# A new instruction order for a fused attention and expert kernel: first values by a casting load, gate steps split from the weight loads, just-in-time loads

## The chip, the cores and the metric

The kernel runs on one core of one Trainium2 chip. The metric is the time of one execution on the device in microseconds (us). Each comparison below runs the kernels on the same chip, beside the kernel before, and states the median and the ratio to the kernel before with its 95% interval. Runs over 1.5% above the fastest of the same kernel are classed slow; the ratios and all profiles are of fast runs alone, while a median can hold a slow run. The profiled run of a kernel has a span that is about 1.6 us shorter than its time (215.1 against 216.68 in the kernel before).

## The reference, cut to what matters

```python
# q, k, v: (8, 8, 576, 64)   w_gate: (512, 8)   w1: (8, 512, 1024)   w2: (8, 1024, 512)
scores = q @ k.T / sqrt(64)                   # per batch and head
mask   = (rel >= 0) & (rel < 64)              # sliding window of 64, causal
attn   = softmax(where(mask, scores, -1e9)) @ v
x      = attn.transpose(0, 2, 1, 3).reshape(8, 576, 512)
e      = argmax(x.mean(axis=1) @ w_gate)      # one expert for a whole batch
out[b] = gate_prob[b] * (relu(x[b] @ w1[e]) @ w2[e])
```

The expert of a batch is known only when the attention of that batch is complete. A batch's expert weights (2 MB for w1 and as much for w2, as fp32) can then be loaded, and only then can its expert matmuls run. So the kernel runs the attention of later batches between the expert matmuls of earlier ones.

## The kernel before

Each engine's order of instructions follows one list of tokens. A "unit" is one fifth of a batch's attention (number = 5 x batch + part; part 4 is the tail of 64 positions). `T` transposes q and k, `U` and `k` copy the transposes out of PSUM (`a` on ACT, `d` on DVE), `S` makes scores (`b`: the mask is added by matmuls; otherwise `K` multiplies by it on DVE), `E` exponentiates on ACT, `l` sums on TensorE, `n` and `R` make the reciprocal on ACT, `A` multiplies by the values and `X` scales on DVE. `g` and `G` make the gate, `H` and `I` its probability. `Q`, `t`, `L` load q/k, tails and values of a batch through the GpSimd queue, `c` is the next expert chunk (most are 8 matmuls of 512 columns), `ra`/`rd` evacuate it, `F` is filler.

```python
OPS = ("F5 Tm0 Ud0 vd0 vd2 Q1 ... X3 X4 g0 Tm12 Ud10 ka9 E7 Ud11 G0 Ud12 V1 ... c ka16 n8 ...").split()

    def load_v0():                 # values of batch 0: fp32 through SP, then cast on DVE or ACT
        for J in range(4):
            nc.sync.dma_start(out=v32[:, J], in_=v[0, :, 128*J:128*J+128].rearrange("h c d -> c h d"))
        ...
    def gate0(b):                  # token g: gate sums on DVE and the gate matmul on PE
        ...
    def gate1(b):                  # token G: the index, then all four weight loads
        nc.vector.max(out=gmx, in_=glog)
        nc.vector.max_index(out=eidx, in_max=gmx, in_values=glog)
        ereg = nc.gpsimd.alloc_register(f"er{b}")
        nc.gpsimd.load(ereg, eidx[0:1, 0:1])          # GpSimd waits here for the gate
        esl = ds(nc.gpsimd.snap(ereg, donate=True), 1)
        ...
        for c in range(2): nc.gpsimd.dma_start(out=w1t[...], in_=w1s[...])
        for c in range(2): nc.gpsimd.dma_start(out=w2t[...], in_=w2s[...])
```

GpSimd issues its loads in order, so while it waits for a batch's index it issues none of the loads listed behind.

The softmax here doesn't subtract the row's maximum and nothing guards it: scores larger than these inputs give would overflow.

Of the kernel before, what the change touches and what calls it, by code (L numbers as in the profile page):

```python
# [1 line left out]
TB=1;MB=3;LO='24.46.68.t';WU=12  # L2
OPS = (
    "F5 Tm0 Ud0 vd0 vd2 Q1 vd4 F5 F2 T1 ka0 Ua1 ka1 Sb0 Tm2 kd2 Ud2 Sbm1 M vd3 va1 E0 Tm3 "
    "l0 V0 E1 Ua3 n0 ka3 Sb2 l1 E2 T4 l2 Sb3 Tm5 Q2 n1 R0 R1 kd4 Ud4 t1 T6 E3 Sb4 Tm7 A0 n2 "
    "ka6 E4 l3 kd5 n3 Ud5 Ud6 T8 Am1 R2 l4 Am2 Sb5 X0 Am3 Sbm6 t2 ka7 n4 E5 kd8 X1 L1 R3 "
    "Ud7 T9 Sb7 F1 Ua8 Am4 Sbm8 Tm10 E6 Q3 T11 X2 Ua9 R4 X3 X4 g0 Tm12 Ud10 ka9 E7 Ud11 G0 "
    "Ud12 V1 Tm13 l5 E8 kd13 l6 Sb9 ka10 H0 kd11 Am5 n5 R5 n6 A6 E9 S10 T14 Ud13 R6 E10 l7 "
    "kd12 S11 n7 Tm15 l8 E11 R7 Ud14 L2 X5 kd14 Am7 S12 T16 c ka16 n8 Ud15 I0 X6 kd15 c K10 "
    "c S13 Am8 l9 T17 A9 Q4 t3 l10 E12 R8 c c c X7 rd K11 Ua16 ra n9 S14 K12 Ua17 R9 n10 "  # L10
    "E13 X8 R10 rd X9 rd c ra l11 c E14 rd n11 ra ra ka17 c c T18 ra g1 V2 G1 H1 S15 c c c "
    "l12 n12 E15 A10 K14 rd kd18 c rd c K15 K13 X10 L3 c R11 Am11 c l13 Ua18 ra R12 T19 X11 "
    "Am12 S16 n13 c l14 Am13 R13 Tm20 I1 rd S17 X12 rd Ua19 E16 X13 c kd20 Ud20 kd19 E17 c "
    "T21 Tm22 S18 l15 A14 n14 c rd t4 c c c ka22 R14 rd Ua21 n15 ka21 X14 Ud22 ra g2 Q5 T23 "
    "c S19 c ra c K17 E18 ra ra G2 rd K16 rd c l16 rd c V3 K18 S20 l17 H2 R15 E19 c rd Am15 "
    "l18 A16 c n16 c n17 ka23 T24 E20 R16 n18 Ud23 I2 X15 K19 l19 A17 S21 ra c c c S22 R17 "
    "A18 Ua24 E21 c X16 T25 X17 R18 kd24 A19 E22 c S23 c L4 t5 X18 ra ra ra n19 c ra c ra "
    "R19 rd c X19 E23 c ra K21 ka25 Ud25 S24 c g3 K20 G3 ra c ra T26 E24 rd kd26 ra c c l20 "
    "c K24 c K22 H3 c Ud26 T27 V4 l21 S25 K23 Ud27 n20 c c c c R20 ra I3 ra n21 T28 l22 Q6 "
    "R21 ra c A20 c ra ra kd27 A21 X20 l23 S26 c c n22 E25 l24 rd X21 A22 R22 c c c c ra "  # L20
    "kd28 rd n23 Ud28 E26 n24 ra T29 A23 L5 rd K25 ra R23 ra ra l25 c A24 X22 R24 n25 X23 "
    "X24 rd c c S27 c g4 K26 c c S28 Ud29 G4 E27 l26 t6 T30 H4 kd29 rd K27 c kd30 rd Ud30 "
    "S29 c c c T31 rd E28 K28 n26 S30 l27 E29 ra V5 A25 R25 R26 c c K29 Ua31 X25 kd31 A26 "
    "ra E30 l28 T32 I4 rd X26 n27 kd32 S31 c rd Ud32 A27 c T33 S32 c rd E31 R27 n28 rd R28 "
    "X27 K31 c ra ra A28 l29 c L6 X28 rd K30 c A29 n29 c ka33 R29 Q7 ra X29 Ud33 rd c c E32 "
    "S33 T34 c c g5 c c G5 ka34 ra E33 Ud34 H5 S34 V6 rd c K33 l30 E34 n30 c K32 l31 A30 c "
    "T35 n31 R30 t7 ra ka35 X30 K34 I5 Ud35 rd l32 n32 c A31 T36 l33 ra S35 rd R31 Ud36 X31 "
    "c c R32 rd ka36 n33 l34 A32 X32 E35 T37 rd Ua37 n34 R33 L7 R34 S36 c c c c A33 ra ra "
    "E36 rd kd37 c X33 rd T38 A34 S37 c c ka38 K36 ra c Ua38 ra X34 g6 c c E37 S38 K35 ra "
    "G6 l35 T39 H6 c c n35 E38 K37 c kd39 R35 ra V7 l36 A35 c l37 A36 n36 Ud39 rd X35 ra "  # L30
    "K38 S39 c R36 A37 l38 n37 c E39 X36 A38 R37 K39 I6 X37 rd rd l39 c n38 c c R38 A39 ra "
    "n39 c c ra R39 X38 X39 ra g7 rd c G7 c c c rd rd c ra rd c c c ra c c c c c c ra ra ra "
    "rd c c H7 I7 ra ra rd c c c c ra c ra ra c c rd rd rd rd c c c c ra rd c c c c rd ra "
    "ra "
# [19 lines left out]
def kernel(  # L54
# [23 lines left out]
    xpool = ctx.enter_context(tc.tile_pool(name="xpool", bufs=3))  # L78
# [19 lines left out]
    def load_qk(b, lo, hi):  # L98
        if lo == 0:
            qkv[b] = (ld.tile([128, H, 256], BF16, tag="qm", name="qm"),  # L100
                      ld.tile([128, H, 256], BF16, tag="km", name="km"),
                      ld.tile([128, H, D], BF16, tag="qkt", name="qkt"))
        qm, km, _ = qkv[b]
        for (t, src) in ((qm, q), (km, k)):
            nc.gpsimd.dma_start(  # L105
                out=t[:, lo:hi],
                in_=src[b, lo:hi, 0:SM].rearrange("h (p r) d -> p h (r d)", r=4))

    def load_tail(b):
        qkt = qkv[b][2]  # L110
        for (p0, src) in ((0, q), (64, k)):
            nc.gpsimd.dma_start(
                out=qkt[p0:p0 + 64],
                in_=src[b, :, SM:S].rearrange("h p d -> p h d"))

    def load_v(b):
        vt = vw[b % NV]
        for J in range(4):
            nc.gpsimd.dma_start(  # L119
                out=vt[:, 2 * J + 1],  # L120
                in_=v[b, :, 128 * J:128 * J + 128].rearrange("h c d -> c h d"))
        nc.gpsimd.dma_start(
            out=vt[64:128, 8], in_=v[b, :, SM:S].rearrange("h c d -> c h d"))

    v32 = const.tile([128, 5, H, D], FP32, tag="vw32", name="vw32")

    def load_v0():
        for J in range(4):
            nc.sync.dma_start(
                out=v32[:, J], in_=v[0, :, 128 * J:128 * J + 128].rearrange("h c d -> c h d"))  # L130
        nc.sync.dma_start(out=v32[64:128, 4], in_=v[0, :, SM:S].rearrange("h c d -> c h d"))

    def cast_v(J, e):
        if J < 4:
            copy(e)(out=vw[0][:, 2 * J + 1], in_=v32[:, J])
        else:
            copy(e)(out=vw[0][64:128, 8], in_=v32[64:128, 4])
# [20 lines left out]
    load_qk(0, 0, 2)  # L158
    load_v0()
# [16 lines left out]
    for c in LO.split("."):  # L176
        if c == "t":
            load_tail(0)
        else:
            load_qk(0, int(c[0]), int(c[1]))  # L180
    nc.gpsimd.affine_select(out=mt, in_=mt, compare_op=ALU.is_ge, fill=0.0,
                            base=64, pattern=[[1, 64]], channel_multiplier=-1)
    nc.gpsimd.affine_select(out=mt, in_=mt, compare_op=ALU.is_ge, fill=0.0,
                            base=-1, pattern=[[-1, 64]], channel_multiplier=1)
# [8 lines left out]
    for t in vw:  # L193
        nc.vector.memset(t[0:64, 0].bitcast(U32), 0)

# [58 lines left out]
    def unit_s(b, i, e):  # L254
        qt = tT.pop((b, i))
        kt = kT[b % 2]
        pm = 'b' in e
        if 'm' in e:
            sp = [ps_m.tile([128, 512], FP32, tag="mo", name="s") for _ in range(2)]
        else:  # L260
            s2 = ps_s.tile([128, 2, 512], FP32, tag="s", name="s")
            sp = [s2[:, 0], s2[:, 1]]
        n = 512 if i < NP else 256
        if pm:
            for hh in range(2):
                nc.tensor.matmul(out=sp[hh][:, 0:n], lhsT=ident, rhs=maskb if i < NP else masktb,
                                 start=True, stop=False, skip_group_check=True)
        for m in range(n // 64):
            for hh in range(2):
                p0 = 64 * hh  # L270
                kq = kt[p0:p0 + 64, i, 64 * m:64 * m + 128] if i < NP else kt[p0:p0 + 64, m, SM:SM + 128]
                nc.tensor.matmul(out=sp[hh][:, ts(m, 64)], lhsT=kq, rhs=qt[p0:p0 + 64, m],  # L272
                                 start=not pm, stop=True, skip_group_check=True)
        sps[b, i] = sp if 'm' in e else [s2[:, :, 0:n]]
# [40 lines left out]
    def unit_a(b, i, e):  # L315
        vt = vw[b % NV]
        if i == 0:
# [54 lines left out]
    gpss = {}  # L372

    def gate0(b):
# [6 lines left out]
                                axis=mybir.AxisListType.X)  # L381
        gps = ps_a.tile([128, E], FP32, tag="lb", name="gps")
# [5 lines left out]
    def gate1(b):  # L388
# [4 lines left out]
        nc.vector.max_index(out=eidx, in_max=gmx, in_values=glog)  # L393
        ereg = nc.gpsimd.alloc_register(f"er{b}")
        nc.gpsimd.load(ereg, eidx[0:1, 0:1])
# [6 lines left out]
        w2s = w2e[esl].squeeze(0)  # L402
        for c in range(2):
            nc.gpsimd.dma_start(out=w2t[:, ts(c, 4)], in_=w2s[:, ts(c, 4)])  # L404
        wts[b] = (w1t, w2t)
        gnm = gpool.tile([128, 1], FP32, tag="gnm", name="gnm")
        nc.vector.tensor_scalar(out=gnm, in0=gmx[:, 0:1], scalar1=-1.0 / S,
                                scalar2=None, op0=ALU.mult)
        gates[b] = (glog, gnm)
# [23 lines left out]
    def w1_chunk(b, ft):  # L433
        xm, xt = xs[b]
        w1t, _ = wts[b]
# [37 lines left out]
    def w2_chunk(b, r, half):  # L473
        hm, ht = hts[b]
        _, w2t = wts[b]
# [20 lines left out]
    def chunks():  # L496
        for b in range(B):
            for ft in range(9):
                yield lambda b=b, ft=ft: w1_chunk(b, ft)
            for r in range(4):  # L500
# [10 lines left out]
                 "Q": lambda b: load_qk(b, 0, 8), "L": load_v, "t": load_tail}  # L511

    with tc.manual_schedule():
        for op in OPS:
# [6 lines left out]
            elif c == "F":  # L521
                wps = ps_m.tile([128, 512], FP32, tag="mo", name="wps")
                for _ in range(int(x)):
                    nc.tensor.matmul(out=wps, lhsT=warm[:, 0:128], rhs=warm, start=True, stop=True)
            elif c == "M":
                tail_mask()
            elif c == "v":
                cast_v(int(x), e)
# [36 lines left out]
```

## Time and profile before

| | before |
|---|---|
| time, median of 3 | 217.01 us (215.91 to 217.77) |
| span of the profiled run | 215.1 us |
| first expert chunk starts | 42.2 us |
| PE busy / idle, from there to its last matmul | 162.8 / 6.0 us |
| last evacuation and store | about 4 us |

The last three rows add up to the span. Most of this document is bookkeeping on them, since TensorE (PE) paces the kernel. The stretch behind the first chunk is this row (PE, PEld, DVE, ACT and POOL busy time with counts, clock, DMA share, GB/s):

```profile
42.20:211.05 168.85, 162.81 (x2928) 105.57 (x2922) 99.30 (x279) 102.65 (x186) 58.43 (x74) 1.00 1.35 202
```

From the page, the chain of work that ended last, by engine, and two rows of the DMA issues (size, then median time from issue to landing):

```profile
PE 48%; DMA 34%; POOL 8%; issue 4%; DVE 2%; POOLq 1%; ACT 0%
...
w1t<-in_moe_w_dram POOLq DMA_DIRECT2D x16, 512.0 KB, 8.9
...
km<-in_k_dram POOLq DMA_DIRECT2D x7, 512.0 KB, 9.8
```

A weight load takes some 9 us in the middle, and a third of the chain already passes through DMA, although PE stands still for only 6 us.

### The profile page before, as it was taken

The numbers are of one execution on the slowest core, as the hardware profiler recorded it, in microseconds if no ns is written. First come the engines' busy times: TensorE is split into PE (matmuls) and PEld (weight loads), VectorE is DVE, ScalarE is ACT, GpSimd is POOL, SyncE is SP. The second block draws the span as 40 slices with busy tenths as digits, with TensorE's granted clock in tenths as the row PEclk, the third lists the DMA queues.
The fourth block names the chain that finished last, engine by engine and source line by source line (L and its number), as shares of the span: only waits on it lengthen the run. The fifth ranks groups of instructions, "written<-read, shape, count | busy, mean of one in ns | idle before, by whom it ended". The sixth has DMA issues, their size and how long they took to land.

```text
span 215.1 us, 8172 instructions
## 1 busy us (share of the span) xinstructions
PE 196.3 (91%) x3545; PEld 126.6 (59%) x3549; DVE 121.5 (56%) x350; ACT 129.6 (60%) x233; POOL 85.1 (40%) x114
## 2 busy tenths in 40 slices
PE   7975977899899999899999999999799999799992
PEld 2443845666576556556565657665567575567761
DVE  4262549892776567156645788757648486402520
ACT  2188588898285938585677466754876684233211
POOL 7993351934391276213831094145531410500000
PEclk9999599999999999999999999999999999999999
DMA  6999999999999999999999999999999999999423
GB/s 131 218 186 198 177 147 143 150 201 167 195 227 242 184 165 202 242 236 181 193 247 235 194 177 235 245 168 188 221 266 200 116 172 278 216 188 254 112 101 122
DMA packets 86036, 41.51 MB, mean 193 GB/s; under 512 B 48112, under 2 KB 81904, under 8 KB 86000
## 3 DMA queue, kind: packets, MB, share of 16 engines
q0 software_dynamic: 74896, 30.35, 116.0%
q1 hardware_dynamic: 11104, 10.64, 16.4%
q8 instruction: 28, 0.46, 0.8%
q14 instruction: 8, 0.07, 0.1%
HBM read 61.88 MB, written 9.44 MB: 332 GB/s over the span
## 4 chain that ended last, share of the span: by engine, by line
PE 48%; DMA 34%; POOL 8%; issue 4%; DVE 2%; POOLq 1%; ACT 0%
PE ph L444 20%; PE po L482 14%; DMA w1t<-in_moe_w_dram 13%; DMA w2t<-in_moe_w_dram 8%; DMA km<-in_k_dram 6%; DMA vw_96<-in_v_dram 6%; PE ph L453 3%; PE tp L223 3%; PE s L272 3%; POOL qm L105 2%; POOL km L105 2%; PE po L491 2%; DMA vw_95<-in_v_dram 1%; PE av L328 1%; POOL vw_96 L119 1%
## 5 line engine op out<-in xcount | busy, mean ns | idle before, releaser
L444 PE MATMUL ph<-xm,w1t 128*64 128x512 f16 x512 | 60.7, 381 | 1.6 <-DMA w1t<-in_moe_w_dram 1.6
L482 PE MATMUL po<-w2t,hm 128*64 128x512 f16 x512 | 60.7, 380 | 1.6 <-DMA w2t<-in_moe_w_dram 1.3
L482 PEld LDWEIGHTS <-hm 128*64 128x64 f16 x512 | 29.6, 110 | 20.8 <-issue 2.2
L444 PEld LDWEIGHTS <-w1t 128*64 128x64 f16 x512 | 29.0, 110 | 21.5 <-DMA w1t<-in_moe_w_dram 2.0
L285 ACT ACTIVATE pe<-s 128x1024 f16<-128x1024 f32 x29 | 29.8, 1028 | 9.9 <-PE s L272 8.6
L431 DVE TENSOR_SCALAR hm<-ph,gw 128x512 f16<-128x512 f32 x30 | 22.3, 747 | 16.7 <-PE ph L444 16.1
L348 ACT ACTIVATE ln<-lb 128x512 f32<-128x512 f32 (+1 forms) x40 | 22.3, 558 | 13.8 <-PE lb L306 13.3
L361 DVE CUSTOM_DVE_ANT_0 xm<-av,rl 128x512 f16<-128x512 f32 x32 | 21.9, 686 | 14.4 <-PE av L328 9.8
L429 ACT ACTIVATE hm<-ph,gw 128x512 f16<-128x512 f32 x34 | 23.0, 690 | 11.5 <-PE ph L444 11.5
L401 POOL DMA_DIRECT2D w1t<-in_moe_w_dram x16 | 12.2, 770 | 39.0 <-DVE hm L431 11.3
L354 ACT ACTIVATE rl<-ln 128x512 f32<-128x512 f32 (+1 forms) x40 | 23.2, 591 | 0.7 <-DVE pool L361 0.6
L463 ACT COPY ob<-po 128x512 f32<-128x512 f32 x19 | 11.0, 586 | 16.1 <-PE po L482 16.1
L294 DVE TENSOR_TENSOR pe<-pe,mask 128x1024 f16<-128x1024 f16 x24 | 16.2, 684 | 1.2 <-ACT pe L285 1.1
L119 POOL DMA_DIRECT2D vw_95<-in_v_dram x12 | 10.6, 886 | 15.2 <-DMA km<-in_k_dram 6.8
L223 PE MATMUL tp<-ident,km 128*64 128x128 bf16 x256 | 13.7, 231 | 2.5 <-DMA km<-in_k_dram 2.5
L463 DVE COPY ob<-po 128x512 f32<-128x512 f32 x13 | 8.9, 681 | 12.4 <-PE po L482 12.4
L306 PE MATMUL lb<-pe,ones 128*64 128x512 f16 x64 | 12.8, 393 | 2.8 <-ACT ln L348 1.9
L223 PE MATMUL tp<-ident,qm 128*64 128x128 bf16 x256 | 13.5, 229 | 0.9 <-DVE qt L239 0.9
L223 PEld LDWEIGHTS <-qm 128*64 128x64 bf16 x256 | 10.2, 116 | 4.5 <-issue 2.2
L239 DVE COPY qt<-tp 128x512 bf16<-128x512 bf16 x22 | 9.2, 419 | 6.2 <-PE tp L223 3.8
L404 POOL DMA_DIRECT2D w2t<-in_moe_w_dram x16 | 12.1, 769 | 0.5 <-issue 0.5
L105 POOL DMA_DIRECT2D qm<-in_q_dram x11 | 9.4, 854 | 6.4 <-DMA w2t<-in_moe_w_dram 4.1
(110 smaller groups left out, 275.7 us busy)
## 6 DMA issues: line engine op xcount, KB each, us to landing
w1t<-in_moe_w_dram POOLq DMA_DIRECT2D x16, 512.0 KB, 8.9
w2t<-in_moe_w_dram POOLq DMA_DIRECT2D x16, 512.0 KB, 15.3
out_dram<-ob SPq DMA_DIRECT2D x32, 256.0 KB, 6.7
qm<-in_q_dram POOLq DMA_DIRECT2D x7, 512.0 KB, 7.2
km<-in_k_dram POOLq DMA_DIRECT2D x7, 512.0 KB, 9.8
vw_95<-in_v_dram POOLq DMA_DIRECT2D x12, 128.0 KB, 14.8
vw_99<-in_v_dram SPq DMA_DIRECT2D x4, 256.0 KB, 5.2
vw_96<-in_v_dram POOLq DMA_DIRECT2D x8, 128.0 KB, 14.0
```

The source lines that it names most:

```text
L105: nc.gpsimd.dma_start(out=t[:, lo:hi], in_=src[b, lo:hi, 0:SM].rearrange("h (p r) d -> p h (r d)", r=4))
L223: nc.tensor.transpose(tp[p0:p0 + 64, n, r], t[:, 2 * i + hh, ts(r, 64)], ident)
L285: nc.scalar.activation(out=po, in_=sp[0], func=AF.Exp, scale=scale)
L294: nc.vector.tensor_tensor(out=pe, in0=pe, in1=mask if i < NP else maskt, op=ALU.mult)
L348: nc.scalar.activation(out=ln, in_=lb[:, 0:n], func=AF.Ln)
L354: nc.scalar.activation(out=rl, in_=lns.pop((b, i)), func=AF.Exp, scale=-1.0)
L361: nc.vector.tensor_tensor_reduce(out=xm[:, i], in0=av.rearrange("q r p -> q (r p)"), in1=rl, scale=1.0, scalar=0.0, op0=ALU.mult, op1=ALU.add,
L429: nc.scalar.activation(out=o, in_=i, func=AF.Relu, scale=g)
L431: nc.vector.tensor_scalar(out=o, in0=i, scalar1=g, scalar2=0.0, op0=ALU.mult, op1=ALU.max)
L444: nc.tensor.matmul(out=ph[64 * c:64 * c + 64], lhsT=w1t[:, kb, ts(2 * ft + c, 64)], rhs=xm[:, kb], start=(kb == 0), stop=(kb == 3), skip_g ...
L463: copy(e)(out=ob, in_=po)
L482: nc.tensor.matmul(out=po[64 * c:64 * c + 64], lhsT=hm[:, fb, ts(2 * r + c, 64)], rhs=w2t[:, fb], start=(fb == 0), stop=(fb == 7), skip_gr ...
```

## The change

The intent seems to be an earlier first chunk and fewer waits. It has five parts. Batch 0's values are loaded as a cast in the GpSimd queue, which removes the fp32 buffer and five casts. The gate is split into steps: `g` (sums), `p` (matmul), `G` (index), `w` (load w1), `y` (load w2). Value loads come in five separately placed pieces, and q/k loads come after the weights of batches two earlier. Full-array mask and filler matmuls become two 64-column halves. Finally all tokens have a new order, with nine mask matmul groups behind the first chunk, where there were none. Two small things come along, a fourth buffer for the attention's output and a later making of the tail mask.

```diff
-    "F5 Tm0 Ud0 vd0 vd2 Q1 vd4 F5 F2 T1 ka0 Ua1 ka1 Sb0 Tm2 kd2 Ud2 Sbm1 M vd3 va1 E0 Tm3 "
... the whole list is replaced
+    "q0.02 F2 L0.1 q0.24 q0.48 t0 Tm0 F3 Ud0 kd0 L0.0 T1 Ua1 kd1 L0.2 Sbm0 F1 E0 L0.4 Sb1 "
...
-    xpool = ctx.enter_context(tc.tile_pool(name="xpool", bufs=3))
+    xpool = ctx.enter_context(tc.tile_pool(name="xpool", bufs=4))
...
-    def load_v0():          # and cast_v: removed
+    def load_v(b, J):       # one piece, by a casting load on GpSimd
...
+    def gate_p(b):          # the gate matmul alone
+    def load_w1(b):         # reads the index, then loads w1
         ereg = nc.gpsimd.alloc_register(f"er{b}")
-        nc.gpsimd.load(ereg, eidx[0:1, 0:1])
+        nc.gpsimd.load(ereg, eidxs[b][0:1, 0:1])
...
+    def load_w2(b):
...
-                nc.tensor.matmul(out=sp[hh][:, 0:n], lhsT=ident, rhs=maskb if i < NP else masktb,
-                                 start=True, stop=False, skip_group_check=True)
+                for c in range(2):
+                    nc.tensor.matmul(out=sp[hh][64 * c:64 * c + 64, 0:n], lhsT=ident[:, ts(c, 64)],
+                                     rhs=maskb if i < NP else masktb,
+                                     start=True, stop=False, skip_group_check=True)
```

## The prediction

> **What bounds the kernel now.** I read the page's busy table first, then the stretches, then the order of instructions on TensorE and GpSimd up to the first weights, then what TensorE waits for.
>
> ```profile
> PE 196.3 (91%) x3545; PEld 126.6 (59%) x3549; DVE 121.5 (56%) x350; ACT 129.6 (60%) x233; POOL 85.1 (40%) x114
> PEclk9999599999999999999999999999999999999999
> HBM read 61.88 MB, written 9.44 MB: 332 GB/s over the span
> ```
>
> PE is the fullest engine; the one weak clock slice is the fifth (about 21 to 27 us). Memory traffic is 71.3 MB, or 8.9 MB for each of the 8 batches. The stretches below give PE, PEld, DVE, ACT and POOL busy time, clock, DMA share and GB/s (which counts written bytes; a cast load writes half of what it reads).
>
> ```profile
> 0.00:42.15 42.15, 33.48 (x623) 20.95 (x629) 22.12 (x72) 26.60 (x46) 26.65 (x41) 0.92 1.36 168
> ...
> 100.00:124.00 24.00, 23.96 (x418) 14.61 (x412) 14.28 (x43) 14.81 (x26) 9.21 (x11) 1.00 1.47 211
> 124.00:147.00 23.00, 23.00 (x462) 15.02 (x460) 16.80 (x45) 15.17 (x26) 10.52 (x13) 1.00 1.60 204
> 147.00:170.00 23.00, 21.37 (x426) 14.10 (x424) 14.95 (x41) 15.15 (x28) 9.08 (x12) 1.00 1.47 213
> ```
>
> From 42.15 on, PE is idle only 6.0 us up to its last matmul at 211 (the idle of all stretches added), and from 100 to 147 not at all. So after the first expert matmul the kernel is paced by PE. Before that it is a start-up of 42 us:
>
> ```profile
> 12.22 1.04 ACT L285 ACTIVATE pe<-s 128x1024 f16<-128x1024 f32 x1
> 32.73 0.22 DVE L367 CUSTOM_DVE_ANT_0 xt<-al,rl 128x64 f16<-128x64 f32 x1
> 34.00 0.26 PE L384 MATMUL gps<-grd,ones_105 128*64 128x8 f32 x4
> 34.85 0.16 DVE L393 FIND_INDEX8 eidx<-gmx,gps 128x8 uint32<-128x8 f32 x1
> 36.77 1.50 POOL L401 DMA_DIRECT2D w1t<-in_moe_w_dram  x2 [6.84 <-DVE vw_95 L141]
> 42.15 1.03 PE L444 MATMUL ph<-xm,w1t 128*64 128x512 f16 x8
> ```
>
> Batch 0's attention runs from its first exponential (12.22) to its last scaling (32.95), mixed with batch 1's; the gate names the expert at 35.0, the load starts 1.8 us later and lands 5.4 us after that. DMA is close behind PE. The weight loads of batches 1 and 5 start at 57.53 and 147.38; four batches of 8.9 MB in 89.85 us are 397 GB/s.
>
> **What the Trainium skill says.** "DMA: Bandwidth & Descriptors", section SWDGE vs HWDGE vs iDMA: a cast in a DMA needs GpSimd. The kernel agrees in form: the first values come over SP as fp32 and are cast on DVE and ACT. "HBM Reference", Specifications (TRN2): a core streaming alone reaches about 425 GB/s; the 397 here sustained leaves at most some 7%. "TensorEngine Tiling (Array Packing)", Key Properties: changing the tiling mode drains TensorE. The trace agrees: after the full-array mask matmul each score group's weight load stands 0.42 us. "TensorE: Matmul & The Clock Gate", Part 1: the clock halves after an idle window of some 3.4 us. The trace shows one slice at half clock, though the longest PE wait near it was only 1.3 us, so it doesn't quite fit.
>
> **The change part by part.**
>
> *PE work.* I cost each step by its start-to-start time in the full stretch: `103.51` to `103.96` is a transpose pair (0.44), scores 0.34 plus some 0.06 of mode change, denominators 0.22, values 0.25; an expert chunk is 0.864 (64 matmuls in 6.91), the tail chunks 1.01 and 0.87. Tails cost about half. A mask matmul pair is 0.43.
>
> Adding these along the old order: 157.9 us of work after the first chunk. Measured: 211 - 42.15 = 168.8, so 6.0 idle plus 4.9 that my unit costs miss (3%). The end then adds 4.2 (last evacuation and store).
>
> In the new order the first chunk comes earlier in the list: only 11 tiles are transposed and 10 scored ahead of it, not 17 and 13. Useful work done before it falls from 15.5 to 11.0 us; so 4.5 to 5 us moves behind it. Also nine score groups behind the first chunk now carry the mask as matmuls (seven full, two tails: 7 x 0.43 + 2 x 0.22 = 3.4 us), against none before. In return DVE loses as many multiplications of 0.68 us, but DVE is at 56%. Work after the first chunk becomes 166.6, and with the 3% it is 171.4.
>
> *Start-up.* The new order puts all of batch 0's attention ahead of batch 1's. GpSimd issues batch 0's q/k (2.36 MB) and v (1.18 MB) first, 13 DMAs at 0.7 to 0.9 us, done by about 13 us. The five SP loads (5.1 us of SP issue) and five casts (0.36 to 0.64 each) go away; they lie beside other work, so I count nothing for them except cleaner queues. What then paces batch 0 is ACT: five exponentials (4 x 1.04 + 0.6), logarithms (4 x 0.6 + 0.4), exponentials of them (4 x 0.62 + 0.46), two copies (1.2): 11.7 us. From 12.2 this gives 23.9, with a microsecond of gaps 25. The last scaling takes it to 25.7, the gate's sums and matmul (32.95 to 34.26 before) to 27, the index to 27.7, and the weight load starts 1.8 later: about 29, against 36.77. Batch 1's q/k must land for the transposes queued ahead of the gate matmul; at 5.6 MB issued and some 350 GB/s (7.1 + 1.2 MB by 26.3 before) that is about 20, in time. Splitting the gate (p, w, y) lets Q2 go between w1 and w2; w1 still lands 5.4 us after its issue, so the first chunk is near 34 (32.5 to 36), 8 us earlier.
>
> *Sum.* 34 + 171.4 + 4.2 = 209.6 plus whatever PE idles; before it was 42.15 + 162.8 + 4.2 + 6.0 = 215.1. So the 8.1 us won at the start are nearly paid back: 4.6 to 5.3 for work only moved, 3.4 for masks. With the old idle of 6.0 the change is worth almost nothing; the gain is what the search took from the idle. The weights are now asked for 6 to 8 us of PE work ahead of their first use (before 5 to 12), but with the queue emptier. A weight load's landing was 5.3 us at best and 8.9 in the middle, plus 1.8 to issue, so waits of 0.5 to 1 us in several batches are to be expected. The old order had 2.9 us of such waits in all. The w2 loads are asked for 12 to 15 us of work ahead (before 15 to 22). I take 2 to 4 us of idle in all: span about 212, and the time stands 1.6 above the span in the profiled run (216.68 against 215.1): 213.3.
>
> **Rivals.** *The search fills everything.* Someone put masks on a full PE, so either DVE's latency before each gate was a wait, or PE would have stood there anyway. Then idle falls to near zero and the start is at its best: 209 to 211. For it: a search is not likely to keep 3.4 us of loss. Against: 6 us of idle is all there is to win. *Just-in-time loads become waits.* A late gate or a 9 us landing costs 1 to 2 us in each of six batches: 216 to 219, no gain. For it: the short distances. Against: loads of q, k and v now come behind the weights. *DMA becomes the bound.* At 397 GB/s a batch costs 22.5 us, and new PE work per batch is some 22.4: equal. Fewer bytes are loaded before the first chunk, so less is in reserve: 213 to 215. *The clock.* If the half-clock window falls on the first chunks, not the start-up, it costs up to 3 us.
>
> **Range and chances.** The middle is 213.3, 1.7% below 217.0; the border of 2% is at 212.7, well inside my uncertainty (first chunk plus or minus 1.5, idle plus or minus 2, unit costs 1). Range 209.5 to 216.8. Faster 0.41, same 0.55, slower 0.04.
>
> **What would show it.** The first weights issue at 28 to 30 us and the first L-line expert matmul at 33 to 36; batch 0's last scaling near 26. PE idle behind the first chunk of 2 to 4 us, most of it released by w1t. Mask matmuls inside the busy stretch, about 3.4 us. Wrong, if the first chunk is still after 38, if idle is above 6 (loads) or under 1 (then under 211), or if a chunk comes to another pace than 0.864 us.

## The result, and the profile after

| | before | after | difference |
|---|---|---|---|
| time, median of 3 | 217.01 | 226.02 | +9.0 |
| ratio | 1 | 1.0416 [1.0321, 1.0511] | slower |
| span | 215.1 | 224.4 | +9.3 |
| first chunk | 42.2 | 34.3 | -7.9 |
| PE busy behind it | 162.8 | 173.4 | +10.6 |
| PE idle behind it | 6.0 | 12.4 | +6.4 |
| end | 4.0 | 4.3 | +0.3 |

A ratio is the mean time of one kernel's fast runs over that of the other's in the same rounds, so it isn't quite the ratio of the medians.

The change is 4.2% slower. From the page of the kernel after, the counterparts of the lines shown above:

```profile
PE 199.4 (89%) x3624; PEld 125.9 (56%) x3624; DVE 122.1 (54%) x342; ACT 132.2 (59%) x235; POOL 88.4 (39%) x117
...
HBM read 61.88 MB, written 9.44 MB: 318 GB/s over the span
...
DMA 47%; PE 32%; issue 8%; POOL 5%; DVE 4%; ACT 2%; POOLq 1%; DVEq 0%
...
w1t<-in_moe_w_dram POOLq DMA_DIRECT2D x16, 512.0 KB, 7.5
...
km<-in_k_dram POOLq DMA_DIRECT2D x7, 512.0 KB, 18.5
```

The bytes are the same. DMA has taken PE's place in the chain, "issue" has doubled, and a k load now takes 18.5 us to land instead of 9.8. It looks as if late q/k loads were the cause; two experiments that issue them earlier did not make the kernel faster. The two stretches, with columns as before:

```profile
0.00:34.20 34.20, 25.91 (x488) 14.94 (x490) 18.33 (x58) 20.56 (x37) 28.78 (x43) 1.00 1.48 143
34.30:220.05 185.75, 173.38 (x3138) 110.94 (x3134) 103.65 (x285) 111.32 (x197) 59.57 (x75) 1.00 1.30 192
```

The start is 8 us shorter, with 488 matmuls in it instead of 623. Behind it PE is busy longer and idle for 185.75 - 173.38 = 12.4 us. What PE waits for behind the first chunk, in the kernel after and then in the one before (us in total, times, longest):

```profile
PE ph L446 <- DMA w1t<-in_moe_w_dram: 3.8, 4, 1.4
PE av L319 <- issue: 1.5, 1, 1.5
PE tp L212 <- issue: 1.2, 1, 1.2
PE tp L212 <- DMA km<-in_k_dram: 1.1, 3, 0.5
PE av L319 <- DVE pool L352: 0.8, 1, 0.8
PE tp L212 <- DVE qt L228: 0.8, 1, 0.8
```

```profile
PE ph L444 <- DMA w1t<-in_moe_w_dram: 1.6, 3, 0.9
PE po L482 <- DMA w2t<-in_moe_w_dram: 1.3, 1, 1.3
PE s L272 <- issue: 1.0, 2, 0.7
PE tp L223 <- DMA km<-in_k_dram: 0.9, 1, 0.9
```

The idle time is scattered, and no single wait in the kernel after is longer than 1.5 us. With the smaller entries that are left out here, the kernel after waits 5.3 us for loads, 3.4 for DVE and 3.6 for "issue"; the kernel before 3.8, 1.1 and 1.0. So waits for loads are only 1.5 of the 6.4 us of added idle time; 2.3 are waits for DVE and 2.6 are "issue". Next, how the gate stands against the first use. These are rows of PE's timeline in the kernel after (start, us, then the idle time before and its releaser):

```profile
77.35 0.29 PE L380 MATMUL gps<-grd,ones 128*64 128x8 f32 x4
...
86.81 1.92 PE L446 MATMUL ph<-xm,w1t 128*64 128x512 f16 x16 [1.36 <-DMA w1t<-in_moe_w_dram]
...
91.54 1.92 PE L446 MATMUL ph<-xm,w1t 128*64 128x512 f16 x16 [0.65 <-DMA w1t<-in_moe_w_dram]
```

and these are of GpSimd's, one weight issue each, the batches 0, 2, 3, 4 and 5:

```profile
26.84 1.52 POOL L404 DMA_DIRECT2D w1t<-in_moe_w_dram  x2 [0.81 <-issue]
...
79.17 1.49 POOL L404 DMA_DIRECT2D w1t<-in_moe_w_dram  x2 [2.17 <-DVE pe L285]
...
103.31 1.49 POOL L404 DMA_DIRECT2D w1t<-in_moe_w_dram  x2 [10.66 <-DVE qtt L232]
...
128.86 1.50 POOL L404 DMA_DIRECT2D w1t<-in_moe_w_dram  x2 [4.03 <-DVE qt L228]
...
152.48 1.50 POOL L404 DMA_DIRECT2D w1t<-in_moe_w_dram  x2 [7.93 <-PE tp L212]
```

In batch 2 the gate matmul starts at 77.35 and the issue at 79.17. PE reaches the first chunk at 86.81 - 1.36 = 85.45, so 6.28 us behind the issue, and the load has not landed. Ahead of the issues of batches 3, 4 and 5 GpSimd stands for 4 to 11 us; the releaser that the row names is only the nearest semaphore event in time, since the instruction that waits there is the read of the gate's index. Read from the same rows for all middle batches of both kernels, in us from the weights' issue until PE has reached the first chunk (a wait is taken off):

| batch | 1 | 2 | 3 | 4 | 5 | 6 | mean |
|---|---|---|---|---|---|---|---|
| before | 7.80 | 11.19 | 9.13 | 7.19 | 8.10 | 7.94 | 8.6 |
| after | 7.01 | 6.28 | 7.44 | 6.59 | 7.99 | 7.03 | 7.1 |

The new order asks for the weights 1.5 us later relative to their first use. But the first chunk needs only the first half of w1, and that half lands sooner too: 6.9 us after its issue in the mean of these batches, 8.0 before. So the margin shrinks by only 0.3 us, from 0.5 to 0.2, and the direct waits for w1 grow only from 1.6 to 3.8 us.

### The profile page after: what moved, and what is told of

Read it like the earlier page. It is cut to its first block, busy times and chain, and to the rows that moved or that the text cites.

```text
span 224.4 us, 8302 instructions
## 1 busy us (share of the span) xinstructions
PE 199.4 (89%) x3624; PEld 125.9 (56%) x3624; DVE 122.1 (54%) x342; ACT 132.2 (59%) x235; POOL 88.4 (39%) x117
## 4 chain that ended last, share of the span: by engine, by line
DMA 47%; PE 32%; issue 8%; POOL 5%; DVE 4%; ACT 2%; POOLq 1%; DVEq 0%
DMA km<-in_k_dram 31%; PE ph L446 10%; PE po L484 8%; DMA w1t<-in_moe_w_dram 8%; DMA w2t<-in_moe_w_dram 7%; PE tp L212 3%; PE av L319 2%; PE s L263 2%; POOL w2t L411 2%; PE lb L297 1%; PE ph L455 1%; POOL qm L110 1%; POOL w1t L404 1%; PE po L493 1%; POOLq L398 1%
## 5 line engine op out<-in xcount | busy, mean ns | idle before, releaser
L484 PE MATMUL po<-w2t,hm 128*64 128x512 f16 x512 | 62.2, 380 | 0.4 <-DMA w2t<-in_moe_w_dram 0.4
L124 POOL DMA_DIRECT2D vw<-in_v_dram x32 | 29.0, 915 | 27.3 <-DMA w2t<-in_moe_w_dram 12.2
L276 ACT ACTIVATE pe<-s 128x1024 f16<-128x1024 f32 x25 | 25.8, 1031 | 13.0 <-PE s L263 13.0
L263 PEld LDWEIGHTS <-kT 64*128 64x128 bf16 x576 | 10.9, 95 | 14.2 <-issue 10.7
L465 DVE COPY ob<-po 128x512 f32<-128x512 f32 x15 | 10.3, 685 | 12.9 <-PE po L484 12.8
L319 PE MATMUL av<-pe,vw 128*64 128x64 f16 x512 | 14.5, 197 | 3.0 <-issue 1.5
L238 DVE COPY kT<-tp 128x512 bf16<-128x512 bf16 x17 | 11.5, 686 | 8.3 <-ACT qt L228 6.9
L319 PEld LDWEIGHTS <-vw 128*64 128x64 f16 x512 | 12.7, 112 | 4.9 <-issue 1.1
L285 DVE TENSOR_TENSOR pe<-pe,mask 128x1024 f16<-128x1024 f16 x20 | 13.5, 687 | 2.8 <-ACT pe L276 2.0
L263 PE MATMUL s<-qt,kT 64*128 64x64 bf16 x512 | 13.1, 191 | 1.9 <-issue 1.3
## 6 DMA issues: line engine op xcount, KB each, us to landing
km<-in_k_dram POOLq DMA_DIRECT2D x7, 512.0 KB, 18.5
```

What stands on the lines that cost most here:

```text
L124: nc.gpsimd.dma_start(out=vt[:, 2 * J + 1], in_=v[b, :, 128 * J:128 * J + 128].rearrange("h c d -> c h d"))
L263: nc.tensor.matmul(out=sp[hh][:, ts(m, 64)], lhsT=kq, rhs=qt[p0:p0 + 64, m], start=not pm, stop=True, skip_group_check=True)
L276: nc.scalar.activation(out=po, in_=sp[0], func=AF.Exp, scale=scale)
L319: nc.tensor.matmul(out=av[p0:p0 + 64, :, 16 * m:16 * m + 16], lhsT=vt[:, m, 2 * i + hh], rhs=pe[:, hh, m], start=(m == 0), stop=(m == 7), ...
L484: nc.tensor.matmul(out=po[64 * c:64 * c + 64], lhsT=hm[:, fb, ts(2 * r + c, 64)], rhs=w2t[:, fb], start=(fb == 0), stop=(fb == 7), skip_gr ...
```

## The experiments

The expectations number the theories. **Theory 1:** the q/k loads, now placed behind weights, come late. **Theory 2:** there is more PE work behind the first chunk. **Theory 3:** DMA as a whole is short. After the first four runs came **Theory 4:** the gate comes late, so weights, and everything that stands behind them in GpSimd's queue, come late; and **Theory 5:** the start-up left too little loaded. Rivals for parts of the loss are the nine masks, the values in line, the halved mask matmuls and the shallower look-ahead.

### Late q/k loads, masks, and the parts put into the kernel before

**a_qearly**: the kernel after, with q/k loads 14 to 29 chunks earlier (not 7 to 28, as the expectation has it).

```diff
-y0 ... Q3 (chunk 14) ... Q4 (35) ... Q5 (53) ... Q6 (71) ... Q7 (88)
+y0 Q3 ... Q4 (chunk 7) ... Q5 (24) ... Q6 (44) ... Q7 (62)
```

> The changed kernel (226.0 us) with the q/k loads of batches 3 to 7 moved 7 to 28 expert chunks earlier, so that each is issued ahead of the weights of its neighbour batch and not behind them; nothing else moves. Theory 1 (late q/k: the chain of the changed kernel rests for 31% of its span on q/k transfers that land 15.7 to 19.3 us after issue, and each holds up transposes, attention, gate and the next weights in turn): landing falls to 7 to 10 us, the weight issues come about 22 us apart and not 25, time 217 to 220. Theory 2 (more PE work behind the first chunk: nine mask matmuls and the attention work moved there): no change, 224 to 227. Theory 3 (DMA as a whole is short): no change, since the same bytes go through; the weights land later instead.

Measured 233.83 us, ratio 1.0839 [1.0732, 1.0946], so 4% slower than the kernel after. Waits of PE:

```profile
PE ph L444 <- DMA w1t<-in_moe_w_dram: 12.7, 4, 10.1
```

The earlier q/k loads took the transfers from batch 1's weights: issued at 53.08, they let the first chunk of the batch start at 66.57 only, after a wait of 10.1 us. The granted clock was at half for 10 us just around the end of this wait (60.2 to 70.4), so a part of the loss may be the clock. Theory 1 falls in this form.

**a_nomask**: the kernel after without the nine mask groups behind the first chunk (a multiplication on DVE in their place).

```diff
-Sb10 ... E10 ...
+S10 ... E10 K10 ...        (the same for units 11, 15, 19, 22, 24, 26, 32, 38)
```

> The changed kernel with the nine mask matmul groups behind the first expert chunk turned back into multiplications on DVE. Theory 2 (PE work is the bound): about 3.4 us less, 222 to 223. Theory 1 or 3 (PE waits for loads anyway): within 1 us of 226.

Measured 224.49 us, 1.0406 [1.0317, 1.0494]. PE's busy time fell by 3.6 us, as the prediction had sized it, but its idle time rose by 2.3. The masks' cost is real work that fills what would otherwise be partly waiting. They are not the main cause; the ratio hardly moves (1.0416 with them).

**b_v0gp**: the kernel before, with batch 0's values loaded as a cast on GpSimd.

```diff
-LO='24.46.68.t'           # values over SP, casts vd0 vd2 vd4 vd3 va1
+LO='v1.24.46.68.t.v0.v2.v4.v3'
```

> The kernel before (217.0 us) with only the first values changed: five cast DMAs on GpSimd in line with q/k, no SP loads and no casts on DVE and ACT. If this part is to blame: 219 or more, with the first expert chunk later than 42.15. If it is neutral, as I hold: 216 to 218.

Measured 219.51 us, 1.0211 [1.0123, 1.03]: slower, by 1.2 to 3.0%. The first chunk moved from 42.2 to 45.1. The first 11 us in the kernel before, then in this one:

```profile
0.00:11.00 11.00, 9.62 (x57) 3.94 (x58) 3.63 (x17) 2.13 (x3) 9.69 (x20) 1.00 1.02 174
```

```profile
0.00:11.00 11.00, 9.62 (x76) 4.14 (x78) 2.90 (x15) 2.69 (x4) 9.70 (x19) 1.00 0.92 94
```

POOL is just as busy (9.7 us), but 94 GB/s move instead of 174. That overstates it: written bytes are counted, and a cast writes half of what it reads. In bytes read it is about 2.1 MB instead of 2.7 (worked out from 0.75 MB written by GpSimd's queue and 1.17 by SP's before, 1.02 and 0.02 here). GpSimd is busy issuing for nearly all of this stretch, and SP had been a second issuer: with the values in line, batch 1's first q load is issued at 13.77 instead of 10.07. The Trainium skill, "DMA: Bandwidth & Descriptors", section Issuing engines are not separate DMA queues, says that issuing from several engines saves only the sequencer's time to initiate the loads, usually small relative to the DMA itself. In this start that saving was worth 2.9 us on the first chunk: PE waited 3.6 us for batch 1's q.

**b_maskcol**: the kernel before with mask and filler matmuls in two halves, as in the diff above.

> The kernel before with only the form of mask matmuls and fillers changed to two 64-column halves. All of them lie ahead of the first expert chunk, so all theories: within 1 us of 217.0; it measures whether the form itself costs or saves.

Measured 215.65 and 213.75 us in its two fast runs, against 215.37 for the kernel before; two more, 217.19 and 219.21, count as slow, and no ratio was made. The busy time behind the first chunk was 162.3 and the idle 6.1. I call it neutral.

### The gate's wait taken away

**a_static**: the kernel after, with expert = batch number instead of the gate's choice. The result is wrong (relative error 1.22). The bytes and the matmuls are the same, but GpSimd waits for no index.

```diff
-        ereg = nc.gpsimd.alloc_register(f"er{b}")
-        nc.gpsimd.load(ereg, eidxs[b][0:1, 0:1])
-        esl = ds(nc.gpsimd.snap(ereg, donate=True), 1)
+        esl = ds(b, 1)
```

> The changed kernel with the expert taken as number b and not as the gate says (a wrong result on purpose): GpSimd no longer waits for the gate before it issues weights; same bytes, same order of issue. Theory 4 (the gate names the expert too late: from the gate's matmul to landed weights it takes 9 to 12 us, and the new order leaves 6 to 8 us of TensorE work for that): the w1t waits of TensorE go, GpSimd's waits of 4 to 11 us ahead of the weights go, time 217 to 221. Theory 3 (DMA as a whole is short): hardly less than 224, since the same bytes come in the same order. Theory 5 (the start-up left too little loaded and the loads are in the wrong order) : below 224 only by what starts earlier, 221 to 224.

Measured 216.22 us, 1.0071 [0.9984, 1.0157]. The wait for the gate's choice costs the new order 3.4 points of the ratio, some 7 us (a repeat below, on one chip, gives 8.9); PE's idle time fell from 12.4 to 6.6 us. The gain is a little more than Theory 4 expected, and Theory 3 falls in this form, since the same bytes came in the same order. Whether it costs the old order as much is asked with b_static.

**a_shift3** and **a_shift6**: all chunks and evacuations come three or six chunks later in the list, so the gate stands further ahead of its use.

```diff
-c  ... c  ... c  ... c  ...      (each c, ra and rd in its place)
+   ...    ...    ... c  ...      (each at the place of the one three, or six, chunks later)
```

> The changed kernel with the stream of expert chunks and their evacuations put three chunks later against everything else, so that each gate stands 2.6 us of TensorE work further ahead of its first chunk. Theory 4: w1t waits fall from 3.8 to about 1 us and the time to 221 to 223. Theory 3: no change.

> The same with six chunks (5.2 us). Theory 4: w1t waits gone, weights about 23 us apart, 218 to 222, less than with three chunks. Theory 3: no change. If the first chunk moves as much later as the waits shrink, both theories give 224 to 226.

Measured 236.99 us, 1.1033 [1.092, 1.1146], and 243.65 us, 1.1381 [1.1253, 1.1509]. The waits for w1 vanish, but PE then waits for DVE, ACT and k: the idle time is 19.8 and 26.3 us. The chunks no longer fall into the gaps of the attention that they filled. These two runs were poor instruments: they suggest that chunks and attention steps are fitted to each other, and say nothing against Theory 4.

**a_v0sp**: the kernel after with batch 0's values over SP and casts on DVE, as before.

```diff
-L0.1 ... L0.0 ... L0.2 ... L0.4 ... L0.3
+load_v0() over SP;  ... kd1 vd0 vd1 ... kd2 vd2 ... kd3 vd3 vd4
```

> The changed kernel with the first values loaded as fp32 over SP and cast on DVE, as before the change. In the kernel before, the opposite edit cost 2.1% (first chunk 45.13 and not 42.15). If the cost of that part carries over: first chunk near 32 and 222 to 223; if what follows the first chunk waits for something else: within 1 us of the changed kernel.

Measured 223.92 us, 1.0427 [1.0337, 1.0517]: no gain. The first chunk came 1 us earlier (33.3). So the values in line delay the first chunk by 3 us in the old start and by 1 us in the new one, and there they cost no time that these runs could tell from noise.

### The gate in the old order, and mixtures of both

**b_static**: the edit of a_static in the kernel before.

> The kernel before with the expert taken as number b and not as the gate says (a wrong result on purpose), as was done to the changed kernel, which gained 3.4% by it. Theory 4 (the changed order lost its time because the gate, with everything behind it in the GpSimd queue, comes too late for the loads): the kernel before has slack there and gains little, 212 to 216. If it gains as much as the changed kernel did (208 or less), the wait for the gate is common to both and does not explain their difference.

Measured 211.59 us, 0.9764 [0.9692, 0.9836]. The old order loses less to the gate: 2.4%, a little more than Theory 4 expected of it.

**b_wlate**: the kernel before, in which GpSimd may issue the weights of batches 1, 2, 3, 4, 6 and 7 only when the chunks are as far as in the new order.

```diff
+        if late:
+            nc.gpsimd.tensor_copy(out=junk, in_=last[0])   # waits for the last evacuation
         ereg = nc.gpsimd.alloc_register(f"er{b}")
```

> The kernel before, its order on TensorE, VectorE and ScalarE as it was, but GpSimd may issue the weights of batches 1, 2, 3, 4, 6 and 7 only once the expert chunks are as far as they are in the changed order (a one-element copy from the last evacuation ahead of the issue). Theory 4: lateness alone costs most of the difference, 219 to 224, w1t waits on TensorE of 3 us or more. If lateness is only a by-product: within 1.5 us of 215 to 217.

Measured 221.73 us, 1.0224 [1.0149, 1.0298]. The waits of PE:

```profile
PE ph L450 <- DMA w1t<-in_moe_w_dram: 8.0, 4, 4.7
```

Later weights alone, in an order that is otherwise the old one, cost 4.8 us of time (216.96 before, on the same chip). This is Theory 4 by itself, though coarsely dosed: one wait alone, in batch 4, is 4.7 us, longer than any in the kernel after.

**a_qahead**: the kernel after with `Q4` to `Q7` three to four chunks ahead of the gate in whose wait they stood (at chunks 27, 45, 64 and 82 instead of 35, 53, 71 and 88).

> The changed kernel with the q/k loads of batches 4 to 7 moved only from just behind the weights of two batches earlier to three to four chunks ahead of that gate, where GpSimd stands idle. Theory 4b (head-of-line: what hurts is that q/k and v stand behind the weights, which stand waiting for the gate): 219 to 222. Theory 4a (what hurts is the landing of the weights themselves): no gain or 1 to 3 us more, as q/k now go ahead of the weights in the transfer queue.

Measured 228.16 us, 1.0564 [1.0484, 1.0644]: no faster than the kernel after, whose interval it overlaps. PE then waits for the values' copies (3.0 and 1.5 us). Moving q/k ahead a little is no cure either.

**h_start**: the new order up to the first weights' load, then the old order.

```diff
-F5 Tm0 Ud0 vd0 vd2 Q1 ... g0 ... G0                        (old start)
+q0.02 F2 L0.1 ... Tm8 L1.4 Tm7 ka8 t2 Q2 g0 ... p0 T5 G0 w0   (new start), then Ud5 Sb5 ... as before
```

> A mixed order in the changed kernel's code: its start up to the first weight issue (batch 0's attention first, without the S7 and U steps of batch 1), then all that is left in the order of the kernel before. Theory 4: with the long look-ahead of the old order kept, most of the earlier first gate is kept too: first weights near 28, first chunk 37 to 41, 212 to 216. If the early start is worth nothing because the loads of batch 2 come later: 217 to 221.

Measured 227.14 us, 1.0495 [1.0425, 1.0565]. The first weights were issued at 26.29, ten microseconds earlier than before, yet the first chunk started at 46.6, so it missed both expectations. The old order puts batch 1's and 2's attention in between, and PE waited for its loads (6.4 us for k, 3.3 for q). This start does not pay in the old order; the new order's early first chunk also rests on less attention ahead of it, which then has to be done behind.

### Masks without the gate, masks in the old order, values ahead

**a_static_nomask**: a_static and a_nomask together (wrong result).

> The changed kernel with the expert taken as number b (wrong result on purpose) and the nine mask matmul groups behind the first chunk back on DVE. With the gate's wait gone, TensorE should be the bound, so the 3.4 us of mask work should now come back in full, unlike in the gated kernel, where 3.6 us less work gave 0 to 1 us: ratio 0.990 to 0.994 to before, against 1.007 with masks. If it stays above 1.003, mask work is not what is left.

Measured 219.6 us, 1.0192 [1.0099, 1.0285]. The 3.4 us did not come back; if anything it is slower than a_static with its masks, though the intervals overlap. Without the masks PE waits 2.4 us for the multiplication on DVE. So the masks about pay for themselves.

**b_mask9**: the kernel before in the form of b_maskcol, with masks by matmul in the same nine units.

> The kernel before (with the mask matmuls in the two-half form, which was neutral) with the same nine score groups masked by matmuls and not on DVE. There TensorE is the bound: plus 3 us, ratio 1.012 to 1.018. If masks shorten the wait for the gate by as much as they cost: 0.998 to 1.005.

Measured 216.27 us, 1.0065 [0.9995, 1.0135], between the two expectations; busy +2.3, idle -2.3 against b_maskcol. In the old order too the masks cost little: at most 1.35%, perhaps nothing.

**b_vahead**: the kernel before with three value loads moved ahead of the gate's wait, into time in which GpSimd stood idle.

```diff
-... G0 ... L2 ...   G4 ... L6 ...   G5 ... L7 ...
+... L2 G0 ...       L6 G4 ...       L7 G5 ...
```

> The kernel before with three value loads (batches 2, 6 and 7) moved in the GpSimd queue ahead of the gate at which GpSimd stands waiting (6.8, 7.0 and 2.7 us in the profile before). If idle transfer time ahead of the gate is worth something: 0.985 to 0.995. If the old order's transfers are not what it waits for: within 0.5%. If values ahead of the weights delay these, as q/k did in the changed kernel: over 1.005.

Measured 227.05 us, 1.0555 [1.0493, 1.0616]. I had expected idle GpSimd time to be free. Rows of GpSimd's timeline in this kernel, then the same issue in the kernel before:

```profile
121.46 0.88 POOL L117 DMA_DIRECT2D vw<-in_v_dram  x1 [2.59 <-DMA w2t<-in_moe_w_dram]
123.83 0.88 POOL L117 DMA_DIRECT2D vw<-in_v_dram  x1 [1.49 <-DMA qm<-in_q_dram]
126.56 1.75 POOL L117 DMA_DIRECT2D vw<-in_v_dram  x2 [1.85 <-DMA km<-in_k_dram]
...
129.50 1.55 POOL L399 DMA_DIRECT2D w1t<-in_moe_w_dram  x2 [0.33 <-issue]
```

```profile
124.13 1.49 POOL L401 DMA_DIRECT2D w1t<-in_moe_w_dram  x2 [7.03 <-DVE ht L431]
```

Each value load waits for earlier transfers to land, and batch 4's weights go out at 129.50 instead of 124.13. PE waits 10.5 us for w1 in all, 6.8 in one piece, and the clock is at half for 6.8 us around its end (135.9 to 142.7), so a part of the loss may be the clock. GpSimd was idle, but the transfers that it had issued weren't done.

### The gate's share, on one chip

**s_after**, **s_a_static** and **s_b_static** are the kernel after, a_static and b_static once more, in five rounds on one chip beside the kernel before (216.46 us there).

> The changed kernel unaltered, for a ratio on the same chip as the next two: 1.035 to 1.048.

> The changed kernel without the wait for the gate (wrong result on purpose), as in a_static. If the gate's wait is half of the difference between the orders: about 0.995. If a quarter: about 1.007.

> The kernel before without the wait for the gate (wrong result on purpose), as in b_static: 0.974 to 0.980. The distance of these two, against the distance of the two gated kernels, is the part that the gate does not explain.

| | gate decides | expert fixed | gate's cost |
|---|---|---|---|
| old order | 216.46 | 212.15, 0.9824 [0.9762, 0.9886] | 4.3 |
| new order | 225.84, 1.0466 [1.0386, 1.0546] | 216.95, 1.0065 [1.0006, 1.0124] | 8.9 |
| difference | 9.4 | 4.8 | 4.6 |

So about half of the loss, 4.6 of 9.4 us, is the gate's wait being dearer in the new order. The other 4.8 us stay when no gate waits. The ratios say the same: the gate costs 4.0 points in the new order and 1.8 in the old, of a distance of 4.7. Each ratio is uncertain by 0.6 to 0.8 points, so the half is rough. In the profiled runs of the new order (s_after and s_a_static), taking the wait away saves 4.7 us of idle time, 2.5 of busy time and 1.3 at the first chunk. The stretches behind the first chunk of s_a_static, then of s_b_static:

```profile
33.70:209.95 176.25, 170.49 (x3138) 110.89 (x3134) 103.06 (x285) 111.14 (x197) 58.72 (x74) 1.00 1.33 202
```

```profile
41.80:205.15 163.35, 161.88 (x2928) 102.53 (x2922) 99.43 (x277) 102.57 (x186) 56.88 (x71) 1.00 1.36 204
```

With the gate's wait gone, the first chunk is 8.1 us earlier and PE's work behind it 8.6 us longer, so these two cancel. What is left is idle time: 176.25 - 170.49 = 5.8 against 1.5 us. Of these 4.3 us, two stalls make 3.1; in s_a_static they are

```profile
47.37 0.38 PE L212 MATMUL tp<-ident,qm 128*64 128x128 bf16 x7 [1.19 <-issue]
...
70.12 0.19 PE L319 MATMUL av<-pe,vw 128*64 128x64 f16 x1 [1.86 <-issue]
```

and the kernel after has them at the same instructions (47.98 and 72.66, 1.17 and 1.49 us). They fall inside a group of matmuls (only 7 of a group's 8 transposes follow, and only the last of 16 value matmuls), where no data are waited for. Counted from the start, they fall behind the 733rd and the 1117th matmul in the kernel after, a_static, a_qearly and a_nomask alike, although in a_nomask the second of them is another instruction, a transpose. The distance of 384 matmuls, each with a weight load, is 768 instructions. The Trainium skill, "Runtime: NRT & Kernel Launch", section Instruction fetch mechanics, says that an engine's instructions are refilled in blocks of 256, at a cost that is mostly hidden; 768 is three such blocks.

The trace settles that these stalls are refills, because it records the refills as transfers: 28 in the whole run, of 16,384 bytes each. The DMA view of s_a_static from 45.1 to 46.1 us, just ahead of the first stall, has one of them:

```profile
q0 software_dynamic: 1155, 0.14, 228.3%
q8 instruction: 1, 0.02, 5.8%
```

It ends at 46.08, and PE goes on at 47.37; the one ahead of the second stall ends at 68.90, and PE goes on at 70.12. In all the traces kept here, every "issue" stall of PE of over 0.3 us lies a multiple of 256 instructions from these two (to within 4, as some records are missing), and it ends 1.2 to 1.6 us after a refill has ended. The stalls come where PE runs through a block fast: the two blocks took 4.3 and 3.4 us, while the refills started 3.5 and 3.3 us into them and took 1.0 us each. So PE stood where it ran through 256 instructions in less time than their successors took to come. Why a refill starts as late as that is not shown, and no run took the refills away. In s_b_static two such stalls (0.40 and 1.07 us) fall ahead of the first chunk. The rest of the idle time in s_a_static is 2.9 us of waits for DVE, where s_b_static has 1.4 us of waits for loads.

No version gave a right result in less time than the kernel before; b_maskcol and b_mask9 cannot be told from it.

## Why the prediction was wrong

It gave 213.3 us (209.5 to 216.8), and 226.02 came. Step by step:

- **Start-up: right in size, in part by luck.** The weights were issued at 26.84, not "about 29", and the half that the first chunk needs landed 5.6 us later, as "5.4" said. But PE came to the first chunk only at 34.3, 1.9 us after the landing. The two errors cancel, and "near 34" is hit to 0.3 us.
- **Work behind the first chunk: right to 2 us.** "171.4" (166.6 with 3% is 171.6) against 173.4. That the gain at the start is paid back was the right mechanism: -7.9 and +10.6 us. The masks were put at 3.4, and a_nomask saved 3.6 of busy time; but its idle time rose by 2.3, and b_mask9 cost at most 1.35%, so most of it was not lost time. Without the gate's wait the difference in busy time is 8.6 us, just what the prediction sized (171.4 - 162.8); so the other 2.0 come and go with that wait. How is not shown.
- **Idle time: the step that failed.** "I take 2 to 4 us of idle in all" is 12.4 in the trace. With the measured idle in its place, and nothing else corrected, the sum gives 209.6 + 12.4 = 222.0 of span; with the measured work 224. The prediction counted one kind of wait, "most of it released by w1t", and sized that kind about right: "0.5 to 1 us in several batches" came as four waits of 3.8 us in all. It left out the rest: 3.6 us of "issue" stalls, which are refills (shown above), 3.4 of waits for DVE, and 1.5 for k and w2. The term came from "the gain is what the search took from the idle": trust that a search must have improved what I could not see. The gate's wait also costs more than the waits that name a weight load: a_static and s_a_static show 8.9 us in all, 4.3 of which the old order pays too.
- **The second rival, turned down, was the nearest.** "Just-in-time loads become waits" (its 216 to 219 too low) came with 1 to 2 us in each of six batches; measured are 3.8 us in four waits, and more behind them. I turned it down because "loads of q, k and v now come behind the weights". They do, and k then lands 18.5 us after its issue instead of 9.8. Moving loads ahead again did not help (a_qearly, a_qahead), so this lateness is not by itself the cause.
- **DMA as a bound, the third rival: not in the mean.** The change moves the same bytes at a lower rate (318 against 332 GB/s), and s_b_static moves them at 341, so the mean rate doesn't set the time. But in a_qearly and b_vahead PE then waited longer for w1 (12.7 and 10.5 us), so single stretches may well be bound by the transfers; no run tests that.
- **The clock: not involved.** It was 1.00 in both stretches after. The slow slice before lies in the start-up; PE was busy for only 1.63 of the 3.40 us ahead of it (17.1 to 20.5), though in no single wait of that length.
- **Not foreseen:** the refill stalls, of which the new order has 3.1 us more behind its first chunk than the old one without the gate's wait.

What stays open: how the gate's wait adds 2.0 us of busy time, why PE waits for DVE in the new order (2.9 us without the gate's wait, where the old order has none), and what delays the refills.

## What to carry to other kernels

When a load depends on a result, count the time from that result through issue and landing to the first use, and compare it with the work that lies in between; here the new order gave a load 1.5 us less lead per batch, in a queue that works in order, and its gate's wait cost 8.9 us instead of 4.3 (that the lead alone did this is not shown). An earlier start that leaves work undone is no gain by itself when one engine paces what follows: write down the first use, the busy time and the idle time behind it as one sum. A chain of waits names the releaser and not the cause (q/k loads here), so take the suspected wait away in both kernels before you believe it. And an "issue" stall in the middle of a group of matmuls is worth a look at the instruction transfers in the trace.

## What the Trainium skill lacked or had wrong

- "Runtime: NRT & Kernel Launch", section Instruction fetch mechanics: "mostly hidden" is too mild for a stream of short matmuls beside busy transfers. Stalls of 1.2 and 1.9 us came back at the same two places, 768 instructions apart, in s_a_static and, with 1.2 and 1.5 us, in the kernel after; each ended 1.2 to 1.4 us after a refill's transfer had ended.
- "DMA: Bandwidth & Descriptors", section Issuing engines are not separate DMA queues: the page says "usually small"; it isn't where a start is paced by issues. Giving up the second issuer moved the first chunk from 42.2 to 45.1 us in the old order (1 us in the new one).
- No page that I read says that an idle GpSimd doesn't mean idle transfers: three value loads put into its idle time cost 5.6%, and batch 4's weights went out at 129.50 instead of 124.13 us (1.6 us of that came from the batches before).
